# Where the block differences of a Fourier layer's first pass are made: in the Fourier layer itself, or one layer earlier on GpSimd

## The chip, the cores and the metric

The kernel runs on one core of a Trainium2 chip. The metric is the device time of one execution in microseconds; the time before is the median of three runs, 2189.78 us (2187.06 to 2193.19). One execution was profiled; it took 2191.25 us, and the span from its first to its last instruction was 2189.5 us. A change of 0.3% is 6.6 us.

## The reference, cut to what matters

Four layers follow each other on x, 2048 rows of 640 columns, in fp32: attention, Fourier, attention, Fourier. Both attention layers have the same weights, both Fourier layers the same matrices.

```python
x = x + A(layernorm(x))      # 32 heads of 20, each row sees itself and the 255 rows before it
x = x + B(layernorm(x))
x = x + A(layernorm(x))
x = x + B(layernorm(x))

def B(x):                    # real part of a Fourier transform along rows and columns
    a = x @ dft_hid_re.T
    b = x @ dft_hid_im.T
    return dft_seq_re @ a - dft_seq_im @ b
```

## The kernel before

Products in fp32 accuracy are made of three products of split operands: each operand is cut into a high part (ScalarE copies it to a rounded type) and a low part (what is left, a subtraction on VectorE or GpSimd). So every block that TensorE multiplies by costs one ScalarE and one VectorE instruction first. All DMAs are issued by SyncE, in one queue, in the order of the program text; the same holds for each engine's instructions, since the kernel is scheduled by hand.

**Attention (layers 1 and 3).** `heads` runs 128 steps, eight groups of four heads by 16 blocks of 128 rows, after a lead of ten steps. A step has two halves. In each, TensorE makes two transposed score blocks (L659) and two row-maximum score blocks (L631), VectorE reduces the latter (L636), ScalarE takes the exponent (L669), and GpSimd zeroes what lies outside the window with two selects (L675, L679). At the step's end TensorE multiplies by the values (L694), for the block whose selects ran one step earlier. Spare TensorE time is filled with the projection to queries and keys (L257). Its results are cut by GpSimd in a queue of jobs, the "pool" lane, which gives out one job each half-step (`tick`): a cast (L552) and two subtractions of 128x256 (L211) for each piece. They are stored to `qk_d` (L524) and loaded back as `qp` and `kp` (L594) some steps ahead of use; the row maxima go the same way in small DMAs (L649). Three tiles `rr` of 128x512 are first used near the end of this stage.

**Fourier (layers 2 and 4).** `seq` runs over units of the product along rows. The matrix is taken in quadrants, halves and eight blocks j of 128 rows; the first pass (half 0, part 0) has units `a1`, `a2`, `b7`, `b5`, `b` and `g`. The first ones run inside the end of the attention layer, as its output rows become ready. Each block holds column groups c0, c1, c2, c3 of 512. The pass needs three differences per block: d0 = c1 - c0, d1 = c2 - c1, d2 = c2 - d0. `load_to` loads blocks ahead, `cut_to` makes the differences and the high and low parts, `x_to` prepares the other operand, and L1415 multiplies.

In layer 2 the differences are made where they are used: `cut_to` for `a1` and `b` and for `g` with j below 3 on VectorE, for `g` from j = 3 on GpSimd (L1344); `staged` makes those of the two `b7` units, one on VectorE and one on GpSimd. So 18 are on VectorE and 6 on GpSimd. Each is then stored to `c_d` in DRAM (`keep`, 24 stores of 256 KB). In layer 4 `sums_kept` is true: nothing is subtracted, `load_to` takes the difference from `c_d` in place of the column group that only the difference needed. The flag is set at the end of the first Fourier layer.

Of the kernel before, what the change touches and what calls it, by code (L numbers as in the profile page):

```python
# [11 lines left out]
OP = mybir.AluOpType  # L12
# [11 lines left out]
NB = S // P  # L24
# [9 lines left out]
AFTER = 4  # L34
RATE = 4
FIRST = 7
LATE = 9
# [27 lines left out]
class Net:  # L65
    def __init__(self, nc, tc, ctx, a):
# [28 lines left out]
        self.cd = dram.tile([3, NB // 2, P, 512], F32, name="c_d")  # L95
        self.sums_kept = False
        self.xs = [dram.tile([S, D], F32, name=f"x_d{i}") for i in range(3)]
# [484 lines left out]
    def pack(self, quad, sb):  # L582
# [21 lines left out]
        return todo  # L604

    def heads(self, xsrc, xdst, hook):
        nc = self.nc
        qp = [t.rearrange("p (z s) -> p z s", z=2) for t in self.qp]
        kp = [t.rearrange("p (z s) -> p z s", z=2) for t in self.kp]
        pool = self.work  # L610
# [165 lines left out]
        for step in range(-LEAD, steps + 1):  # L776
# [4 lines left out]
            if step + LEAD == steps + 1:  # L781
                for b in ROLES["w"]:
                    self.ring6.pop(b, None)
            self.wide, self.lead, self.tiled = step + LEAD > steps, step < -2, step < steps - 1
            for f in later.pop(step, []):
                f()
            s, t, v = step + LEAD, step, step - 1
            if due and s >= due[0][0]:
# [3 lines left out]
                q, j = (s + AHEAD) // 16, (s + AHEAD) % 16 // 4  # L792
# [238 lines left out]
    def late(self, xsrc, xdst, hook):  # L1031
        nc = self.nc
# [29 lines left out]
        for t in range(NB):  # L1062
            sb, i = t // 4, t % 4
            y = self.y_part(t)
# [7 lines left out]
            else:  # L1072
                for hf, cs in enumerate(both):
                    p = self.bank("o", 320)
# [12 lines left out]
                out=st[1][:, 1:2], in0=st[1][:, 0:1], in1=self.half, op=OP.pow))  # L1087
# [105 lines left out]
    def take_fourier(self):  # L1193
# [6 lines left out]
        p = [cuts(t, 512) for t in self.pt]  # L1200
# [16 lines left out]
        self.acc = {}  # L1217
        self.leaving, self.keeping = [], []

# [61 lines left out]
    def staged(self, u, stage, eng=None):  # L1281

        j, out = self.order[u][3], self.cut_of.setdefault(u, [])
        p, q = cuts(self.raw_of[u], 512)
        if stage == 0:
            if not self.kept_sum(u):
                eng.tensor_tensor(out=p, in0=q, in1=p, op=OP.subtract)
                self.keep(u, p)
            return
        c = self.ring.popleft()  # L1290
        self.ring.append(c)
        self.split(c[0], c[1], (q, p)[stage - 1])
        out.append(c)
        if stage == 1:
            self.kept[j] = c

    def cut_to(self, n):
        nc = self.nc
        while self.n_cut <= min(n, len(self.order) - 1):
            u = self.n_cut  # L1300
# [3 lines left out]
            ph, j = self.order[u][2:]  # L1304
            if ph == "b7":
                if j:
                    self.staged(u, 0, nc.gpsimd)
                    self.staged(u, 1)
                    self.staged(u, 2)
# [11 lines left out]
            if ph in ("a", "a1"):  # L1321
                eng = nc.vector if ph == "a1" else nc.gpsimd
                if not self.kept_sum(u):
                    eng.tensor_tensor(out=t1, in0=q, in1=p, op=OP.subtract)  # L1324
                    if ph == "a1":
                        self.keep(u, t1)
                src = [p] + ([t1] if ph == "a" else [])
            elif ph == "a2":
                src = [t1]
            elif ph == "b5":  # L1330
                self.cut_of[u] = [self.kept.pop(j)]
                continue
            elif ph == "b":
                if not self.kept_sum(u):
                    nc.vector.tensor_tensor(out=p, in0=q, in1=p, op=OP.subtract)
                    self.keep(u, p)
# [46 lines left out]
    def seq(self, n):  # L1383
        nc = self.nc
        sb, part, ph, j = self.order[n]
        for f in self.keeping:
            f()
        self.keeping.clear()
        self.load_to(n + 3 + (ph == "a1" and len(self.raws) > 5))
# [184 lines left out]
    def fourier(self, xsrc, xdst, more):  # L1574
# [205 lines left out]
        for g in range(NB // 2):  # L1780
# [84 lines left out]
```

## Time and profile before

| | us |
|---|---|
| median of three runs | 2189.78 |
| profiled execution, whole | 2191.25 |
| its span | 2189.5 |
| TensorE busy | 2119.5 (97%) |
| VectorE busy | 1600.5 (73%) |
| ScalarE busy | 1139.8 (52%) |
| GpSimd busy | 958.5 (44%) |

Layer 1's steps run from 161 to 530 us, layer 2's products along rows from 543 to 974 us, layer 3's steps from 1252 to 1623 us, layer 4's products from 1634 to 2056 us. Engines are called PE (TensorE), DVE (VectorE), ACT (ScalarE), POOL (GpSimd) and SP (SyncE, which here only issues DMAs) in the rows. In rows of the timeline the columns are the start in us from the span's start, the length in us, engine, line, operation, the tile written and those read; what stands in brackets at the end is how long the engine was idle before, and what ended that. In rows of windows they are the stretch and its length, then for each engine its busy time and number of instructions, then the granted TensorE clock, the share of the DMA engines that was busy, and GB/s.

### The profile page before, as it was taken

Reading aid. Unit: us, or ns where it says so; the run is one execution under the profiler, and the core shown is the slowest. Engines: PE = TensorE matmul, PEld = TensorE weight load, DVE = VectorE, ACT = ScalarE, POOL = GpSimd, SP = SyncE. Lnnn points to the kernel's source line nnn. Section 1 sums busy time; section 2 is a strip of 40 time slices with the busy share of each in tenths; the row PEclk is TensorE's granted clock in tenths of the full one; section 3 lists DMA queues with packets and bytes.
Section 4 is the critical chain, followed back from the end, with each engine's and each line's share of the span. In section 5 each row is a group of like instructions: output and inputs, shape, how many; then the busy total and the mean of one; then the engine's idle time right before and its main releaser. Section 6 shows DMA issues by size and latency. Waiting matters only on the chain.

```text
span 2189.5 us, 48923 instructions
## 1 busy us (share of the span) xinstructions
PE 2119.5 (97%) x17872; PEld 1785.8 (82%) x17872; DVE 1600.5 (73%) x3931; ACT 1139.8 (52%) x2125; POOL 958.5 (44%) x1562
## 2 busy tenths in 40 slices
PE   7999999898999999999999999998999999999999
PEld 7987777677878888889999877776778888888899
DVE  6358888786897868786661588887867968687766
ACT  3117777656554545452341277776566645455332
POOL 3037776765513232332330376767655023241324
PEclk9999999999999999999999999999999999999999
DMA  5546666785566454656646566667855454546653
GB/s 183 175 156 190 199 180 210 213 222 172 200 192 188 129 183 140 212 185 200 205 156 177 161 187 196 186 204 208 216 165 180 141 187 135 166 152 209 225 166 126
DMA packets 227088, 398.40 MB, mean 182 GB/s; under 512 B 39968, under 2 KB 86560, under 8 KB 226848
## 3 DMA queue, kind: packets, MB, share of 16 engines
q1 hardware_dynamic: 226848, 395.28, 57.8%
q8 instruction: 141, 2.31, 0.5%
q14 instruction: 99, 0.81, 0.1%
HBM read 273.94 MB, written 120.06 MB: 180 GB/s over the span
## 4 chain that ended last, share of the span: by engine, by line
PE 79%; DVE 6%; DMA 4%; ACT 4%; POOL 3%; issue 2%; SPq 1%; ACTq 0%; DVEq 0%; POOLq 0%
PE banks L1415 29%; PE banks L239 15%; PE banks L257 12%; PE banks L694 6%; PE banks L659 5%; PE banks L1703 5%; PE banks L631 5%; DVE banks L636 1%; DMA qp<-qk_d 1%; ACT pt L669 1%; DVE qp L232 1%; PE banks L341 1%; DMA qk_d<-c 1%; ACT big L1038 1%; SPq L594 1%
## 5 line engine op out<-in xcount | busy, mean ns | idle before, releaser
L636 DVE CUSTOM_DVE_ANT_0 banks<-banks,mask 128x384 f32<-128x384 f32 (+2 forms) x1024 | 527.1, 556 | 121.4 <-PE banks L631 98.6
L669 ACT ACTIVATE pt<-banks 128x768 f32<-128x768 f32 (+2 forms) x512 | 393.5, 771 | 170.7 <-PE banks L659 59.8
L675 POOL TENSOR_SCALAR_AFFINE_SELECT pt<-pt 128x256 f32<-128x256 f32 x512 | 213.8, 418 | 220.3 <-ACT pt L669 201.6
L257 PE MATMUL banks<-big,wc 64*128 64x512 f32 x1920 | 271.4, 394 | 0.4 <-DVE pt L442 0.4
L659 PE MATMUL banks<-qp,kp 61*128 61x384 f32 (+2 forms) x1024 | 211.4, 382 | 24.2 <-DVE mc L636 17.0
L631 PE MATMUL banks<-kp,qp 60*128 60x384 f32 (+2 forms) x1024 | 206.9, 348 | 8.8 <-DVE mc L636 8.5
L694 PE MATMUL banks<-pt,vq 128*32 128x128 f32 x5760 | 211.2, 278 | 3.5 <-ACT pt L669 3.5
L257 PEld LDWEIGHTS banks<-big,wc 64*128 64x128 f32 x1920 | 187.3, 186 | 22.2 <-ACT x L544 1.3
L679 POOL TENSOR_SCALAR_AFFINE_SELECT pt<-pt 128x256 f32<-128x256 f32 x448 | 193.8, 433 | 0.0
L226 ACT ACTIVATE qp<-pt 128x512 fp32r<-128x512 f32 (+1 forms) x200 | 123.1, 625 | 129.3 <-DVE pt L1346 50.2
L232 DVE TENSOR_TENSOR qp<-pt,qp 128x512 fp32r<-128x512 f32 (+1 forms) x198 | 156.3, 797 | 40.9 <-ACT qp L226 39.3
L694 PEld LDWEIGHTS banks<-pt,vq 128*32 128x32 f32 x5760 | 142.2, 110 | 51.5 <-issue 36.2
L659 PEld LDWEIGHTS banks<-qp,kp 61*128 61x128 f32 x1024 | 108.6, 185 | 88.8 <-DVE mc L636 65.8
L1415 PE MATMUL banks<-qp,big 128*128 128x512 f32 x648 | 153.6, 391 | 0.1
L631 PEld LDWEIGHTS banks<-kp,qp 60*128 60x128 f32 x1024 | 124.7, 187 | 33.7 <-DVE mc L636 21.8
L1344 POOL TENSOR_TENSOR pt<-pt,pt 128x512 f32<-128x512 f32 x32 | 46.2, 1445 | 232.5 <-DMA pt<-c 146.0
L226 ACT ACTIVATE c<-pt 128x512 fp32r<-128x512 f32 x146 | 90.4, 625 | 108.2 <-POOL pt L1324 56.4
L636 DVE DVE_READ_ACCUMULATOR2_ANT mc<- 128x1 f32 x1024 | 144.3, 141 | 0.0
L1415 PEld LDWEIGHTS banks<-qp,big 128*128 128x128 f32 x648 | 120.8, 188 | 24.9 <-POOL qp L232 0.9
L232 DVE TENSOR_TENSOR c<-pt,c 128x512 fp32r<-128x512 f32 x144 | 116.6, 813 | 26.7 <-ACT c L226 24.1
L1415 PE MATMUL banks<-qp,xc 128*128 128x512 f32 x480 | 118.2, 394 | 3.6 <-DVE xc L232 2.1
L552 POOL CAST c<-x 128x512 fp32r<-128x512 f32 x64 | 38.9, 611 | 166.5 <-ACT x L544 162.3
(253 smaller groups left out, 4477.0 us busy)
## 6 DMA issues: line engine op xcount, KB each, us to landing
pt<-c SPq DMA_DIRECT2D x166, 512.0 KB
qk_d<-c SPq DMA_DIRECT2D x80, 512.0 KB
kp<-qk_d SPq DMA_DIRECT2D x384, 80.0 KB
qp<-qk_d SPq DMA_DIRECT2D x384, 80.0 KB
kp<-u_d SPq DMA_DIRECT2D x32, 640.0 KB
o_d<-ou SPq DMA_DIRECT2D x64, 256.0 KB
x_d<-x SPq DMA_DIRECT2D x48, 320.0 KB
v_d<-pt SPq DMA_DIRECT2D x16, 768.0 KB
```

Source lines behind the costliest of these rows:

```text
L226: nc.scalar.activation(hi, src, AF.Copy, scale=-1.0 if neg else 1.0)
L232: (eng or nc.vector).tensor_tensor(out=lo, in0=src, in1=hi.bitcast(F32), op=OP.subtract)
L239: self.nc.tensor.matmul(p, x, y, start=n == 0, stop=n == last)
L257: self.nc.tensor.matmul(ps[a], x[r], y[r], start=half + i == 0, stop=half == 1 and i == n - 1, skip_group_check=True)
L631: nc.tensor.matmul(p, qp[quad % 2][b:b + 60, z, qb * P:(qb + 1) * P], kp[quad % 2][b:b + 60, z, k0 * P:(qb + 1) * P], start=True, stop=True)
L636: nc.vector.tensor_tensor_reduce(out=p, in0=p, in1=self.mask[:, 384 - n * P:], scale=1.0, scalar=NEG, op0=OP.add, op1=OP.max, accum_out=mc ...
L659: nc.tensor.matmul(self.banks[:, banks[e], :n * P], kp[quad % 2][b:b + 61, z, kb * P:(kb + 1) * P], qp[quad % 2][b:b + 61, z, kb * P:(kb + ...
L669: nc.scalar.activation(pt[quad, kb][:, 2 * z:2 * z + 2, :n * P], self.banks[:, b0:b1 + 1, :n * P], AF.Exp, scale=SCALE)
L675: nc.gpsimd.affine_select(out=t[:, :, 0:P], in_=t[:, :, 0:P], pattern=[[0, 2], [1, P]], compare_op=OP.is_ge, fill=0.0, base=0, channel_mul ...
L679: nc.gpsimd.affine_select(out=t[:, :, 256:384], in_=t[:, :, 256:384], pattern=[[0, 2], [-1, P]], compare_op=OP.is_gt, fill=0.0, base=0, ch ...
L694: nc.tensor.matmul(self.banks[32 * h:32 * h + 32, bank, :P], vq[:, 96 * (kb % 4) + 21 * h:96 * (kb % 4) + 21 * h + 32], t[:, h, (qb - kb) ...
L1415: nc.tensor.matmul(self.banks[:, bk, :], p, b[q], start=start and m == 0, stop=stop and last and m == 2, skip_group_check=True)
```

## The change

`differences_at` is new and is called at the start of each step of `heads`. In layer 1 (`ready` is 0 there) and for steps 0 to 79, ten steps are a turn and each turn serves one block j: at its steps 0, 1 and 2 it loads c0, c1, c2 into the three `rr` tiles (256 KB each), at step 4 it puts six subtractions of 128x256 into the pool lane, which make d0, d1 and d2 in place, and at step 8 it stores the three to `c_d`. Layer 2 then does what layer 4 did before: `kept_sum` no longer asks for the flag, `keep` and its stores are gone, `staged` has two stages in place of three, and the `a2` units load d0.

```diff
+TURN = 10
+    def differences_at(self, step):
+
+        j, at = divmod(step, TURN)
+        if not (0 <= j < NB // 2 and self.ready == 0):
+            return
+        c = self.rr
+        if at < 3:
+            self.nc.sync.dma_start(c[at], self.a["c"][0, 0, j][:, at * 512:(at + 1) * 512])
+        elif at == 4:
+            for out, x, y in ((0, 1, 0), (1, 2, 1), (2, 2, 0)):
+                for cs in (slice(0, 256), slice(256, 512)):
+                    self.job("pool", "cd", lambda out=out, x=x, y=y, cs=cs: self.nc.gpsimd.tensor_tensor(
+                        out=c[out][:, cs], in0=c[x][:, cs], in1=c[y][:, cs], op=OP.subtract))
+        elif at == 8:
+            self.flush("cd")
+            for k in range(3):
+                self.post(k, lambda k=k: self.nc.sync.dma_start(self.cd[k, j], c[k]))
...
             self.wide, self.lead, self.tiled = step + LEAD > steps, step < -2, step < steps - 1
+            self.differences_at(step)
...
-                self.post(3, lambda u=u: self.staged(u, 0, nc.vector))
-                self.post(6, lambda u=u: self.staged(u, 1))
-                self.post(9, lambda u=u: self.staged(u, 2))
+                self.post(6, lambda u=u: self.staged(u, 0))
+                self.post(9, lambda u=u: self.staged(u, 1))
...
     def kept_sum(self, u):
-        return self.sums_kept and self.order[u][:2] == (0, 0)
-
-    def keep(self, u, t):
-
-        sb, part, ph, j = self.order[u]
-        if not self.sums_kept and sb + part == 0:
-            kind = {"a1": 0, "b": 1, "b7": 1, "g": 2}[ph]
-            self.keeping.append(lambda: self.nc.sync.dma_start(self.cd[kind, j], t))
+        return self.order[u][:2] == (0, 0)
...
             if ph in ("a", "a1"):
-                eng = nc.vector if ph == "a1" else nc.gpsimd
-                if not self.kept_sum(u):
-                    eng.tensor_tensor(out=t1, in0=q, in1=p, op=OP.subtract)
-                    if ph == "a1":
-                        self.keep(u, t1)
+                if ph == "a":
+                    nc.gpsimd.tensor_tensor(out=t1, in0=q, in1=p, op=OP.subtract)
...
                 if not self.kept_sum(u):
                     nc.vector.tensor_tensor(out=p, in0=q, in1=p, op=OP.subtract)
-                    self.keep(u, p)
...
-                eng = nc.vector if self.order[u][:2] == (0, 0) and j < 3 else nc.gpsimd
                 if self.kept_sum(u):
                     t1, p = p, t1
                 else:
-                    eng.tensor_tensor(out=t1, in0=p, in1=t1, op=OP.subtract)
-                    self.keep(u, t1)
+                    nc.gpsimd.tensor_tensor(out=t1, in0=p, in1=t1, op=OP.subtract)
...
-        self.ready, self.hid, self.sums_kept = 8, False, True
+        self.ready, self.hid = 8, False
```

Two places show what moves. The first is GpSimd's queue in layer 1, at step 5, before. `pt` is the tile with the exponents, L675 and L679 are the two selects, L552 and L211 are the jobs for one piece of the projection (`x` its raw copy, `c` its parts).

```order
L552 CAST c<-x 128x512
L675 AFFINE_SELECT pt_96<-pt_96 128x2x128
L679 AFFINE_SELECT pt_96<-pt_96 128x2x128
L211 TENSOR_TENSOR c<-x,c 128x256
L675 AFFINE_SELECT pt_96<-pt_96 128x2x128
L679 AFFINE_SELECT pt_96<-pt_96 128x2x128
L211 TENSOR_TENSOR c<-x,c 128x256
L675 AFFINE_SELECT pt_97<-pt_97 128x2x128
L679 AFFINE_SELECT pt_97<-pt_97 128x2x128
```

And the same place with the change, where L693 and L697 are the selects and L617 the new subtractions on the `rr` tiles:

```order
L552 CAST c<-x 128x512
L693 AFFINE_SELECT pt_96<-pt_96 128x2x128
L697 AFFINE_SELECT pt_96<-pt_96 128x2x128
L617 TENSOR_TENSOR rr_101<-rr_102,rr_101 128x256
L693 AFFINE_SELECT pt_96<-pt_96 128x2x128
L697 AFFINE_SELECT pt_96<-pt_96 128x2x128
L617 TENSOR_TENSOR rr_101<-rr_102,rr_101 128x256
L693 AFFINE_SELECT pt_97<-pt_97 128x2x128
L697 AFFINE_SELECT pt_97<-pt_97 128x2x128
L617 TENSOR_TENSOR rr_102<-rr_103,rr_102 128x256
```

The new jobs stand one to a half-step, between the selects. In this turn the two subtractions that finish the piece come six half-steps later than before. In each of the eight turns the six new jobs stand directly beside the six jobs of two projection pieces, so that twelve half-steps in a row carry a job, where six did.

The second place is VectorE in layer 2's first pass, units `b` with j = 2 and 3, before. L1335 is the difference, L232 writes low parts (`qp`, `rr`, `c`), L1174 and L1175 make sums of the other operand.

```order
L1335 TENSOR_TENSOR pt_97<-pt_97 128x512
L232 TENSOR_TENSOR qp_105<-pt_97,qp_105 128x512
L232 TENSOR_TENSOR c<-pt_97,c 128x512
L232 TENSOR_TENSOR rr_8425<-big_6078,rr_8425 128x128
L232 TENSOR_TENSOR qp_8428<-s_7213,qp_8428 128x256
L232 TENSOR_TENSOR qp_8428<-kp_8060,qp_8428 128x256
L1174 TENSOR_TENSOR big_5880<-big_5880 128x256
L1175 TENSOR_TENSOR kp_8060<-big_6078,big_5880 128x256
L1335 TENSOR_TENSOR pt_95<-pt_95 128x512
```

And with the change (L1192 and L1193 are those sums):

```order
L232 TENSOR_TENSOR qp_105<-pt_97,qp_105 128x512
L232 TENSOR_TENSOR c<-pt_97,c 128x512
L232 TENSOR_TENSOR rr_8514<-big_6174,rr_8514 128x128
L232 TENSOR_TENSOR qp_8517<-s_7309,qp_8517 128x256
L232 TENSOR_TENSOR qp_8517<-kp_8145,qp_8517 128x256
L1192 TENSOR_TENSOR big_5976<-big_5976 128x256
L1193 TENSOR_TENSOR kp_8145<-big_6174,big_5976 128x256
L232 TENSOR_TENSOR rr_8516<-pt_95,rr_8515 128x512
```

One instruction of each unit is gone, and the rest keeps its order. TensorE's own order is the same in both kernels from end to end.

More of the change, by code (lines that the diff above doesn't have):

```diff
@@ L95, in __init__ @@
         self.cd = dram.tile([3, NB // 2, P, 512], F32, name="c_d")
-        self.sums_kept = False
         self.xs = [dram.tile([S, D], F32, name=f"x_d{i}") for i in range(3)]
@@ L1217, in take_fourier @@
         self.acc = {}
-        self.leaving, self.keeping = [], []
+        self.leaving = []
     def take_rest(self):
@@ L1271, in kept_sum, with staged @@
     def kept_sum(self, u):
-        return self.sums_kept and self.order[u][:2] == (0, 0)
-    def keep(self, u, t):
-        sb, part, ph, j = self.order[u]
-        if not self.sums_kept and sb + part == 0:
-            kind = {"a1": 0, "b": 1, "b7": 1, "g": 2}[ph]
-            self.keeping.append(lambda: self.nc.sync.dma_start(self.cd[kind, j], t))
-    def staged(self, u, stage, eng=None):
+        return self.order[u][:2] == (0, 0)
+    def staged(self, u, stage):
         j, out = self.order[u][3], self.cut_of.setdefault(u, [])
         p, q = cuts(self.raw_of[u], 512)
-        if stage == 0:
-            if not self.kept_sum(u):
-                eng.tensor_tensor(out=p, in0=q, in1=p, op=OP.subtract)
-                self.keep(u, p)
-            return
         c = self.ring.popleft()
         self.ring.append(c)
-        self.split(c[0], c[1], (q, p)[stage - 1])
+        self.split(c[0], c[1], (q, p)[stage])
         out.append(c)
-        if stage == 1:
+        if stage == 0:
             self.kept[j] = c
@@ L1306, in cut_to @@
                 if j:
-                    self.staged(u, 0, nc.gpsimd)
+                    self.staged(u, 0)
                     self.staged(u, 1)
-                    self.staged(u, 2)
                 continue
@@ L1335, in cut_to @@
                     nc.vector.tensor_tensor(out=p, in0=q, in1=p, op=OP.subtract)
-                    self.keep(u, p)
                 src = [q, p]
@@ L1385, in seq @@
         sb, part, ph, j = self.order[n]
-        for f in self.keeping:
-            f()
-        self.keeping.clear()
         self.load_to(n + 3 + (ph == "a1" and len(self.raws) > 5))
```

1 line of the change is left out of this document (removed).

## The prediction

> **What bounds the kernel now.** First the page's busy shares and the chain that ended last:
>
> ```profile
> PE 2119.5 (97%) x17872; PEld 1785.8 (82%) x17872; DVE 1600.5 (73%) x3931; ACT 1139.8 (52%) x2125; POOL 958.5 (44%) x1562
> PE 79%; DVE 6%; DMA 4%; ACT 4%; POOL 3%; issue 2%; SPq 1%; ACTq 0%; DVEq 0%; POOLq 0%
> ```
>
> TensorE bounds the whole, and the change touches none of its instructions. So it can only gain where TensorE waits or runs slowly for VectorE, and only lose where the moved work makes it wait.
>
> The program holds its own comparison. Layer 4's first pass already runs without subtractions, and with the change layer 2's has the same instructions on every engine. So I cut the pass at the same TensorE instructions in both layers: the first `a1` product, the last one that shares TensorE with attention, the first `b` product of j = 2, the first `g` product, and `g` of j = 2. The windows of layer 2, then of layer 4:
>
> ```profile
> 543.26:594.39 51.13, 48.37 (x266) 42.95 (x265) 43.74 (x117) 28.62 (x53) 28.38 (x36) 1.00 0.68 229
> 594.39:613.65 19.26, 16.63 (x69) 11.91 (x67) 15.95 (x34) 10.81 (x26) 8.14 (x8) 1.00 0.31 101
> 613.65:635.78 22.13, 22.13 (x91) 16.52 (x91) 21.44 (x49) 12.14 (x31) 0.00 (x0) 1.00 0.67 212
> 635.78:649.82 14.04, 12.00 (x44) 8.79 (x42) 12.67 (x19) 9.51 (x18) 1.83 (x1) 0.88 0.61 191
> ...
> 1633.85:1683.07 49.22, 48.11 (x267) 43.05 (x266) 41.20 (x112) 28.73 (x53) 28.34 (x36) 1.00 0.65 213
> 1683.07:1700.77 17.70, 16.16 (x68) 12.16 (x67) 13.64 (x32) 10.87 (x27) 6.54 (x7) 1.00 0.36 108
> 1700.77:1721.62 20.85, 20.70 (x92) 16.83 (x90) 19.74 (x46) 14.42 (x34) 0.00 (x0) 1.00 0.56 174
> 1721.62:1731.14 9.52, 9.52 (x44) 7.89 (x42) 7.90 (x14) 6.98 (x14) 0.00 (x0) 1.00 0.48 143
> ```
>
> The second number is the stretch's length. In the third stretch VectorE is busy 21.44 of 22.13 us in layer 2: it sets the pace there, and the same products take 20.85 us in layer 4. The waits of the first and last stretches, from TensorE's timeline in layer 2 and in layer 4:
>
> ```profile
> 569.61 2.02 PE L239 MATMUL banks<-qp,kp 128*128 128x320 f32 x12 [1.75 <-DVE x L1077]
> 638.50 1.62 PE L1415 MATMUL banks<-qp,vq 128*128 128x512 f32 x6 [0.53 <-ACT kp L1481]
> 642.89 3.79 PE L1415 MATMUL banks<-qp,xc 128*128 128x512 f32 x9 [1.39 <-ACT xc L226]
> ...
> 1658.29 2.02 PE L239 MATMUL banks<-qp,kp 128*128 128x320 f32 x12 [0.64 <-DVE x L1077]
> ```
>
> Layer 4 has the first one shorter, 0.64 in place of 1.75 us, and the other two not at all. Layer 2's last stretch also ran at a mean granted clock of 0.88.
>
> **What the change removes.** Stretch by stretch, layer 2 less layer 4: 51.13 - 49.22 = 1.91, 19.26 - 17.70 = 1.56, 22.13 - 20.85 = 1.28, 14.04 - 9.52 = 4.52; together 9.27 us. Of the 4.52, some 0.12 x 14.04 = 1.7 us is the slower clock, the rest waits. As a check, one of the 18 subtractions on VectorE and the instruction after it:
>
> ```profile
> 611.98 0.69 DVE L1335 TENSOR_TENSOR pt<-pt 128x512 f32<-128x512 f32 x1
> 612.64 0.69 DVE L232 TENSOR_TENSOR qp<-pt,qp 128x512 fp32r<-128x512 f32 x1
> ```
>
> One occupies VectorE from 611.98 to 612.64, so 18 x 0.66 = 11.9 us leave it, against 93.80 - 82.47 = 11.3 us by the sums of the windows. That 9.27 of about 11.9 us reach TensorE is plausible, since VectorE is the late one in all four stretches. The 24 stores also leave layer 2; its loads keep their bytes. I take all 9.27. The low bound of the gain is the third stretch alone, 1.28 us, the only one in which VectorE is visibly full; the high bound is the 11.9 us.
>
> No row tells that the waits made the clock fall; layer 4, without them, shows 1.00 at the same products, so I count the 1.7 us as gained and keep the other case as a rival. The Trainium skill, TensorE: Matmul & The Clock Gate, Part 1, says that the clock falls to half after an idle window of about 3.4 us. By that rule waits of at most 1.39 us would not be the cause, the dip could stay, and the sum would be 1.7 us less.
>
> **What it adds in layer 1: GpSimd.** All in the stretch of steps 1 to 79, 166 to 380 us. Its window, then GpSimd's groups there:
>
> ```profile
> 166.00:380.00 214.00, 211.46 (x3013) 161.16 (x3012) 176.94 (x668) 155.00 (x286) 153.03 (x356) 1.00 0.63 194
> ...
> L675 POOL TENSOR_SCALAR_AFFINE_SELECT pt<-pt 128x256 f32<-128x256 f32 x158 | 64.2, 406 | 60.3 <-ACT pt L669 56.2 <-PE banks L694 2.6 <-PE banks L659 0.9
> L211 POOL TENSOR_TENSOR c<-x,c 128x256 fp32r<-128x256 f32 x40 | 29.6, 739 | 0.0
> ```
>
> The 48 new jobs have L211's shape: 48 x 0.739 = 35.5 us, so GpSimd goes from 153 to 188.5 of 214 us (88%). What hides them is its idle time of 60.3 us before L675. Whether it does so at each place, GpSimd's timeline shows, a stretch with jobs:
>
> ```profile
> 217.48 0.41 POOL L675 TENSOR_SCALAR_AFFINE_SELECT pt<-pt 128x256 f32<-128x256 f32 x1
> 217.84 0.41 POOL L679 TENSOR_SCALAR_AFFINE_SELECT pt<-pt 128x256 f32<-128x256 f32 x1
> 218.21 0.74 POOL L211 TENSOR_TENSOR c<-x,c 128x256 fp32r<-128x256 f32 x1
> 218.91 0.41 POOL L675 TENSOR_SCALAR_AFFINE_SELECT pt<-pt 128x256 f32<-128x256 f32 x1
> 219.26 0.73 POOL L679 TENSOR_SCALAR_AFFINE_SELECT pt<-pt 128x256 f32<-128x256 f32 x1
> 219.95 0.61 POOL L552 CAST c<-x 128x512 fp32r<-128x512 f32 x1
> 220.50 0.40 POOL L675 TENSOR_SCALAR_AFFINE_SELECT pt<-pt 128x256 f32<-128x256 f32 x1
> ```
>
> Counted from start to start, a subtraction takes 0.70, a cast 0.55 to 0.6, and each select 0.36. Twelve half-steps in a row now carry jobs: 24 x 0.36 + 10 x 0.70 + 2 x 0.6 = 16.8 us. TensorE gives them 12 x 214 / 158 = 16.3 us (L675 stands once in each half-step). So GpSimd falls up to 0.6 us behind in each turn, and recovers in the four free steps. The selects' reader is L694, one step later. The tightest place, a group's first block, on GpSimd and on TensorE:
>
> ```profile
> 208.21 0.41 POOL L675 TENSOR_SCALAR_AFFINE_SELECT pt<-pt 128x256 f32<-128x256 f32 x1 [0.52 <-ACT pt L669]
> 209.93 0.42 PE L694 MATMUL banks<-pt,vq 128*32 128x128 f32 x8
> ```
>
> The select ends at 208.62, its reader starts at 209.93: 1.3 us in hand against 0.6 lost. Cost: nothing. Without that cover each turn would cost its lag.
>
> What is late next is a projection piece whose jobs wait six half-steps, about 8 us; its store and the loads after it move with it. That takes us to the queue.
>
> **What it adds in layer 1: DMAs.** 24 loads and 24 stores of 256 KB, 12.6 MB over 214 us, 59 GB/s beside 194. Of SyncE's timeline and waits:
>
> ```profile
> 209.73 0.48 SPq L712 DMA_DIRECT2D o_d<-ou  x1
> 213.91 1.09 SPq L649 DMA_DIRECT2D qp<-mt  x2
> 380.78 1.40 SPq L649 DMA_DIRECT2D qp<-mt  x2
> ...
> SPq L649 <- ACT mt L647: 16.0, 11, 2.4
> ...
> GB/s 187 107 241 203 174 147 282 217 193 118 241 217 169 98 286 222 179 125 248 208 194 87 273 250 206 82 258 185 190 112 228 272 185 125 263 193 207 67 223 286
> ```
>
> The sum of 253 GB/s is below the 286 that single slices reach. Issuing them costs 48 x 0.48 = 23 us of SyncE's time, 0.5 us for each DMA that stands ahead of another. Behind the three stores of a turn stand the small `mt` loads and the `qp` loads. For `mt` SyncE itself waited in eleven cases, 16.0 us in all, so as a rule it is ahead. The readers on TensorE of the two `mt` above start here:
>
> ```profile
> 221.77 0.44 PE L659 MATMUL banks<-qp,kp 61*128 61x384 f32 x2 [0.23 <-DVE mc L636]
> 384.73 0.44 PE L659 MATMUL banks<-qp,kp 61*128 61x384 f32 x2 [0.36 <-DMA qp<-qk_d]
> ```
>
> So 221.77 - 215.0 = 6.8 us are in hand as a rule, and 384.73 - 382.2 = 2.5 us at the worst place, less the landing. Three stores ahead take 1.4 us from it, and a projection store of 1.09 us leaves the place ahead of it. Low bound 0; high bound 2 us per turn, if a store's whole landing came ahead of `mt` each time, 16 us. I take 0.5 us, near the low end, since one place of eight is tight.
>
> **The sum.** Against the profiled execution, 2191.25 us (span 2189.5): -9.27 + 0 + 0.5 = -8.8, that is 2182.5. The median of the runs is 1.5 us lower than that execution, so 2189.8 - 8.8 = **2181 us**, 0.4% faster. Layer 4 and layer 3 do the same as before and only start earlier.
>
> **The rivals.**
> - *The clock dips all the same.* Then 9.27 - 1.7 = 7.6 us are gained, less 0.5: 2182.7. For it: the waits are short. Against it: the mean of 1.00 in layer 4.
> - *Only VectorE's own pace is gained.* The waits of the last stretch end on ScalarE by the rows above. If that stretch gives nothing, 9.27 - 4.52 = 4.75 remain, less 0.5: 2185.5. Against it: layer 4 has none of these waits with the same ScalarE work.
> - *The DMAs show.* SyncE's head waits for a slow store in half of the turns, 1 us each and 2 us more at the tight place: 6 us back, 2186.5. For it: 253 of 286 GB/s leaves little room.
> - *GpSimd falls behind* (slower). In the fence above a select took 0.73 instead of 0.41 at 219.26. If the new jobs stretched as much, 0.32 each, a turn would lose 0.6 + 12 x 0.32 = 4.4 us, of which 1.3 are covered: 3.1 x 8 = 25 us back, 2206. It decides from a job of about 0.75 us start to start: (16.3 - 8.6) / 12 = 0.64 is free, and 1.3 / 12 = 0.11 more is in hand. Against it: the 40 such jobs of this stretch have a mean of 739 ns in all, 0.70 from start to start.
> - *The change does nothing*: excluded, the order shows the subtractions gone.
>
> The Trainium skill, GPSIMD Engine Reference, section 1, says GpSimd shares its SBUF interfaces with VectorE and contends with VectorE instructions that read two SBUF inputs. In these steps VectorE mostly reduces scores out of PSUM (L636, with one mask in SBUF), so by that rule too such stretching stays rare.
>
> **How the numbers follow.** Forecast 0.55, the clock's dip 0.10, VectorE's pace only 0.12, DMAs 0.15, GpSimd 0.08. The forecast's own spread is some 3 us either way, from the clock, which may dip elsewhere, and from runs that spread by 6 us. The range takes in the three middle rivals and leaves out the slower one: 2176 to 2189. A change of 0.3%, 6.6 us, is about what can be told from none; that bound is 2183.2. Of the forecast's 0.55 about 0.47 lies beyond it, of the dip's 0.10 0.06, of the other two 0.04 each: faster 0.61, the same 0.31, slower 0.08.
>
> **What would show it.** Right: layer 2's first pass from its first `a1` product to `g` of j = 2 in about 97.3 us; no clock below 1.00 there; layer 1 from the first to the 80th step within 1 us of now; GpSimd near 188 us in that window. Wrong: L694 waiting for GpSimd, L659 for `qp<-mt`, or L552 in layer 1 waiting for a store.

## The result, and the profile after

The changed kernel takes 2201.86 us (median of four runs, 2201.24 to 2203.23) against 2188.68 for the kernel before (four runs, 2187.06 to 2193.19): a ratio of 1.0054, 95% interval 1.0035 to 1.0072. It is slower by half a per cent, where 0.4% faster was forecast. The profiled execution took 2201.24 us, 9.99 more than that of before.

The busy shares and the chain that ended last, from the page of the changed kernel:

```profile
PE 2120.5 (96%) x17872; PEld 1788.6 (81%) x17872; DVE 1582.6 (72%) x3913; ACT 1140.6 (52%) x2125; POOL 979.9 (45%) x1604
PE 74%; DMA 8%; DVE 6%; ACT 4%; POOL 4%; issue 3%; SPq 2%; ACTq 0%; DVEq 0%; POOLq 0%
```

VectorE lost 17.9 us of work, as meant. The chain shows the other side: TensorE's share fell from 79% to 74%, that of DMA rose from 4% to 8%.

Layer 2's first pass, in the windows between the same TensorE instructions as before (length, then busy time of PE, PEld, DVE, ACT, POOL, the clock, DMA share, GB/s):

```profile
566.90:615.45 48.55, 47.91 (x267) 43.05 (x265) 40.45 (x110) 28.46 (x53) 27.74 (x36) 1.00 0.65 212
615.45:633.28 17.83, 16.17 (x68) 12.16 (x67) 13.63 (x32) 11.01 (x27) 6.68 (x7) 1.00 0.32 107
633.28:654.13 20.85, 20.70 (x92) 16.82 (x90) 19.83 (x46) 14.42 (x34) 0.00 (x0) 1.00 0.54 171
654.13:663.65 9.52, 9.52 (x44) 7.89 (x42) 7.90 (x14) 6.98 (x14) 0.00 (x0) 1.00 0.51 150
```

Together 96.75 us, against 106.56 before: the gain is 9.8 us in these two executions, and the clock is at 1.00 throughout. The loss is in layer 1. Its stretch from the first score product of step 0 to that of step 80, before and after:

```profile
161.18:379.48 218.30, 214.90 (x3038) 163.63 (x3036) 181.03 (x683) 157.15 (x288) 156.32 (x363) 1.00 0.63 194
...
161.58:399.31 237.73, 223.29 (x3038) 169.75 (x3037) 181.31 (x683) 157.22 (x288) 187.98 (x411) 0.96 0.73 225
```

The same 3038 products take 19.4 us more, and the mean granted clock is 0.96. TensorE's longest waits there, in total, times and longest, before (166 to 380 us) and after (166 to 400 us), then three stretches of the changed kernel that follow the long ones:

```profile
PE banks L659 <- DVE mc L636: 2.3, 8, 0.4
...
PE banks L677 <- DMA qp<-mt: 10.3, 4, 3.1
...
238.10:241.50 3.40, 3.40 (x19) 2.69 (x22) 1.71 (x7) 1.35 (x2) 1.47 (x3) 0.50 0.71 212
320.00:326.80 6.80, 6.21 (x49) 5.24 (x51) 1.67 (x11) 2.57 (x5) 2.92 (x6) 0.50 0.78 197
357.50:364.40 6.90, 6.14 (x41) 4.97 (x43) 2.56 (x9) 2.57 (x5) 3.10 (x7) 0.51 0.65 174
```

Before, no product waits for `mt` there. After, score products wait four times for `qp<-mt`, 10.3 us, and there are 17.1 us at half the clock right behind three of these waits, which cost some 8.5 more (half of 17.1; TensorE's busy time grew by 8.4): 18.8 of the 19.4. The first of these waits, on ScalarE, SyncE and TensorE, and the issue and the reader of the same piece before the change:

```profile
226.11 0.25 ACT L665 ACTIVATE mt<-banks 16x128 fp32r<-16x128 f32 x1
...
232.77 1.33 SPq L667 DMA_DIRECT2D qp<-mt  x2
...
237.61 0.44 PE L677 MATMUL banks<-qp,kp 61*128 61x384 f32 x2 [3.09 <-DMA qp<-mt]
...
225.14 1.10 SPq L649 DMA_DIRECT2D qp<-mt  x2
...
232.42 0.44 PE L659 MATMUL banks<-qp,kp 61*128 61x384 f32 x2
```

`mt` is finished at 226.36 and issued at 232.77: it is 6.4 us behind. Before the change the same piece had 6.2 us in hand (232.42 - 226.24), out of which its landing had to come: here the score starts 3.5 us after the issue's end. SyncE's own waits for `mt` show that this is no single accident; they were 16.0 us in eleven cases before:

```profile
SPq L667 <- ACT mt L665: 2.8, 2, 1.9
```

In nearly every group of steps SyncE now arrives late. What is lost by step 80 grows to 23.2 us at the start of layer 2; 9.8 come back there. The last 3.8 aren't shown to be the change's: l2_only below, which adds nothing to layer 1, loses 3.9 between step 80 and layer 2 as well. Layer 3 took 3.6 us less than in the profiled execution before, mostly at steps 96 to 104, where the clock fell in that one and not in this; I put this part down to the run and not to the change, since layer 3's instructions are the same.

### The profile page after: what moved, and what is told of

Its sections match the earlier page's. It is cut to its first block, busy times and chain, and to the rows that moved or that the text cites. A ratio compares the mean times of both kernels' runs of the same rounds, so it can differ in the third digit from the quotient of the medians.

```text
span 2199.5 us, 49035 instructions
## 1 busy us (share of the span) xinstructions
PE 2120.5 (96%) x17872; PEld 1788.6 (81%) x17872; DVE 1582.6 (72%) x3913; ACT 1140.6 (52%) x2125; POOL 979.9 (45%) x1604
## 4 chain that ended last, share of the span: by engine, by line
PE 74%; DMA 8%; DVE 6%; ACT 4%; POOL 4%; issue 3%; SPq 2%; ACTq 0%; DVEq 0%; POOLq 0%
PE banks L1411 30%; PE banks L239 14%; PE banks L257 11%; PE banks L1699 5%; PE banks L712 5%; PE banks L677 4%; PE banks L649 4%; DMA qp<-qk_d 1%; DMA qk_d<-c 1%; DMA qp<-mt 1%; ACT pt L687 1%; DVE banks L654 1%; DMA rr<-r_d 1%; POOL pt L693 1%; SPq L594 1%
## 5 line engine op out<-in xcount | busy, mean ns | idle before, releaser
L654 DVE CUSTOM_DVE_ANT_0 banks<-banks,mask 128x384 f32<-128x384 f32 (+2 forms) x1024 | 527.2, 557 | 140.5 <-PE banks L649 117.3
L693 POOL TENSOR_SCALAR_AFFINE_SELECT pt<-pt 128x256 f32<-128x256 f32 x512 | 213.9, 418 | 204.7 <-ACT pt L687 183.7
L712 PE MATMUL banks<-pt,vq 128*32 128x128 f32 x5760 | 211.4, 278 | 3.5 <-ACT pt L687 3.5
L697 POOL TENSOR_SCALAR_AFFINE_SELECT pt<-pt 128x256 f32<-128x256 f32 x448 | 191.4, 427 | 0.0
L232 DVE TENSOR_TENSOR qp<-pt,qp 128x512 fp32r<-128x512 f32 (+1 forms) x197 | 155.6, 797 | 40.4 <-ACT qp L226 39.0
L712 PEld LDWEIGHTS banks<-pt,vq 128*32 128x32 f32 x5760 | 142.3, 110 | 51.5 <-issue 35.8
L232 DVE TENSOR_TENSOR c<-pt,c 128x512 fp32r<-128x512 f32 x146 | 115.3, 793 | 26.1 <-ACT c L226 23.6
L1328 POOL TENSOR_TENSOR pt<-pt 128x512 f32<-128x512 f32 x30 | 42.7, 1424 | 161.5 <-DVE pt L1345 99.8
```

Of the source, the lines that this page charges most:

```text
L232: (eng or nc.vector).tensor_tensor(out=lo, in0=src, in1=hi.bitcast(F32), op=OP.subtract)
L654: nc.vector.tensor_tensor_reduce(out=p, in0=p, in1=self.mask[:, 384 - n * P:], scale=1.0, scalar=NEG, op0=OP.add, op1=OP.max, accum_out=mc ...
L693: nc.gpsimd.affine_select(out=t[:, :, 0:P], in_=t[:, :, 0:P], pattern=[[0, 2], [1, P]], compare_op=OP.is_ge, fill=0.0, base=0, channel_mul ...
L697: nc.gpsimd.affine_select(out=t[:, :, 256:384], in_=t[:, :, 256:384], pattern=[[0, 2], [-1, P]], compare_op=OP.is_gt, fill=0.0, base=0, ch ...
L712: nc.tensor.matmul(self.banks[32 * h:32 * h + 32, bank, :P], vq[:, 96 * (kb % 4) + 21 * h:96 * (kb % 4) + 21 * h + 32], t[:, h, (qb - kb) ...
```

## The experiments

Theories: **A**, SyncE's queue falls behind with the added transfers; **B**, GpSimd's subtractions hold up the projection's pieces and the stores; **C**, only both together. "Stretch" is the time from step 0's first score to step 80's, against 218.30 before. "Behind" is the mean, over the 16 `mt` of steps 16 to 79, of the time from the end of `mt` on ScalarE to its first issue; it was 0.09 us before. Single times stand beside one run of the kernel before on the same chip. Where that is 2189.28, it is the median of 23 runs.

**The two halves apart.**

> The kernel before with all of the added work in layer 1 (24 loads, 48 subtractions, 24 stores, these into a DRAM tensor of its own), while layer 2 still makes its own differences. If the two halves of the change are independent, layer 1's steps 0 to 96 lose 22 us or so against before (21 to 24, as the changed kernel's trace has it), layer 2's first pass gains nothing, and the time is about 2189 + 23 = 2212 us. If the loss needs layer 2's changed form, the time stays near 2190.

```
 # the kernel before, plus differences_at as in the change, storing to
+self.ed = dram.tile([3, NB // 2, P, 512], F32, name="e_d")
```

2214.19 against 2188.85. Stretch +22.5; layer 2's first pass took 104.9 us, 1.6 us shorter than before, about what the fall of the clock there had cost: its last stretch took 12.40 us in place of 14.04, at a clock of 1.00, although the differences are still made in it.

> The changed kernel without any of the added work in layer 1; layer 2 and layer 4 load blocks of the cosine matrix where the differences would stand (so the output is another one, the bytes loaded are the same). Theory: layer 2's gain stands by itself, 9 to 10 us: 2179 to 2181 us. Rival: part of the 9.9 us that layer 2 gained after the change is only a recovery of what layer 1's delay had left late; then 3 to 6 us are gained, 2184 to 2187.

```
-            self.differences_at(step)
-                self.nc.sync.dma_start(self.t1[j], self.cd[0, j])
+                self.nc.sync.dma_start(self.t1[j], self.a["c"][0, 0, j][:, 512:1024])
-                    self.nc.sync.dma_start(p, self.cd[1 + (ph == "g"), j])
+                    self.nc.sync.dma_start(p, self.a["c"][0, 0, j][:, 0:512])
```

This kernel multiplies by other blocks, so its output is another one. 2182.21 against 2188.85, 6.6 us less, which lies between the two ranges expected. Layer 2's first pass took 9.8 us less than before, but 3.9 us were lost between step 80 and layer 2, where the clock fell twice (at 431.6 and 527.2 us) and in the profile before once (at 432.6). So the gain stands by itself, and so does the loss in the heads.

**Which part of layer 1's work.**

> The kernel before with the 24 loads and 24 stores in layer 1 alone, no subtractions (what is stored are the loaded blocks, into a DRAM tensor that nobody reads). Theory A, SyncE's queue falls behind because 48 more transfers are issued and awaited there: most of the loss, 12 to 23 us, is here, mt is issued 3 to 7 us after it is made, and scores wait for qp<-mt. Theory B, the subtractions on GpSimd delay the projection's pieces and hold the stores: under 5 us lost here. Theory C, only both together: under 5 us here and under 5 us with the subtractions alone.

```
 # l1_all without
-        elif at == 4:
-            for out, x, y in ((0, 1, 0), (1, 2, 1), (2, 2, 0)):
...
```

2214.65 against 2188.85. Stretch +18.1, behind 4.2 us: theory A.

> The kernel before with the 48 subtractions on GpSimd in layer 1 alone (on tiles that VectorE fills once), no loads and no stores. Theory A (SyncE's queue): within 2 us of before, GpSimd at about 188 us busy in the 214 us of steps 1 to 79, mt issued as soon as it is made. Theory B (GpSimd's jobs delay the pieces): 12 us or more lost. Theory C: under 5 us lost.

```
 # l1_all without the loads and stores; at step 0 instead
+            for t in c:
+                self.nc.vector.memset(t, 1.0)
```

2208.07 against 2188.85, not the 2188 of theory A; but `mt` was 0.2 us behind, so not theory B either. Of the stretch's +9.4 us, 2.9 stem from my filling of the tiles at 164 us. The rest is one stall, looked at below.

**Issues or bytes.**

> The kernel before with the same 48 transfers in layer 1 at the same places of SyncE's queue, but only 16 of the 512 columns each (8 KB instead of 256 KB); no subtractions, and nobody reads what is stored. With whole blocks the same 48 transfers cost 24.6 us up to layer 1's 96th step. Theory A1, the time that SyncE needs to issue them (0.4 to 0.5 us each, 20 us in all) puts mt late: still 15 us or more lost, mt issued 4 to 7 us after it is made. Theory A2, the bytes count (a transfer waits for the landing of the eighth before it, which large neighbours delay): under 5 us lost, mt issued under 2 us after it is made as a rule.

```
-            self.nc.sync.dma_start(c[at], self.a["c"][0, 0, j][:, at * 512:(at + 1) * 512])
+            self.nc.sync.dma_start(c[at][:, :16], self.a["c"][0, 0, j][:, at * 512:at * 512 + 16])
 # and the stores alike, in l1_dma
```

2194.19 against 2189.31. Stretch +3.2, behind 2.5 us. The issues alone use up what `mt` had in hand, but hardly more; the bytes make the larger part of the loss. It isn't the landing of `mt` itself that the bytes delay: by the trace's landing records its transfers landed 3.4 us after their issue began in both kernels (medians of the stretch; 2.9 before).

> The changed kernel with one load and one store of 768 KB for each block in place of three and three of 256 KB: 16 transfers in place of 48, the same bytes, a third of the issues and of the places in the queue. Theory A1 (issue time): most of layer 1's loss is gone, 2182 to 2188 us. Theory A2 (bytes): layer 1 still loses 15 us or more, 2195 to 2202 us.

```
-        if at < 3:
-            self.nc.sync.dma_start(c[at], self.a["c"][0, 0, j][:, at * 512:(at + 1) * 512])
+        if at == 1:
+            self.nc.sync.dma_start(self.rr_all, self.a["c"][0, 0, j][:, :1536])
 # and one store of 768 KB
```

2197.72 against 2189.31. Stretch +13.5, behind 4.1 us, with a third of the issues. How bytes reach `mt`, SyncE's timeline and its waits in this kernel show (of rows with x3, three transfers in a row):

```profile
371.55 0.40 SPq L618 DMA_DIRECT2D rr<-c  x1
372.00 1.11 SPq L599 DMA_DIRECT2D kp<-qk_d  x3
373.15 1.09 SPq L599 DMA_DIRECT2D qp<-qk_d  x3
374.35 0.34 SPq L644 DMA_DIRECT2D vq<-v_d  x1
379.09 1.07 SPq L599 DMA_DIRECT2D qp<-qk_d  x2
...
SPq L599 <- DMA rr<-c: 15.0, 6, 4.4
```

The `qp` load at 379.09 reads and writes nothing that the `rr` load touches. It is the eighth transfer after it, and SyncE stood still for 4.4 us until that one had landed. Six such waits, each eight places behind an `rr` load, make the 15.0 us. The trace's semaphore records tell why eight. All transfers of the program report their landing on eight semaphores in turn, and a transfer that waits so waits for the semaphore on which it will report itself: the `rr` load and the `qp` load at 379.09 both have number 105. So this is how the program's transfers are synchronised; no run shows the queue of the chip to have such a limit.

**Another queue.**

> The changed kernel with the two small mt transfers of each group of four steps (in layers 1 and 3) issued by ScalarE, which makes mt, instead of by SyncE. If mt's place behind others in SyncE's queue is what stops the scores, no score waits for qp<-mt any more, layer 1 takes as long as before or less, and layer 2's 9.9 us remain: 2176 to 2182 us. Rival: the queue's delay then shows at the next reader, the loads of queries and keys, or ScalarE loses 1 us per group by issuing: 2190 us or more.

> The kernel before with mt issued by ScalarE, nothing else. Control for the last one: it tells what moving mt gives without the change. Before, only one score waited for mt (1.71 us at 432.96, with a fall of the clock just after): 0 to 5 us faster, 2184 to 2189 us; if ScalarE's issuing costs exps their lead, slower, 2192 us or more.

```
-                self.post(1, lambda z=z: nc.sync.dma_start(
+                self.post(1, lambda z=z: nc.scalar.dma_start(
                     qp[quad % 2][60:125:64, z, u * 512:(u + 1) * 512].bitcast(F32),
```

2311.94 and 2281.87 against 2189.31. In the latter `mt` is never behind, and yet:

```profile
181.44 1.08 ACTq L649 DMA_DIRECT2D qp<-mt  x2
...
183.50 0.38 PE L631 MATMUL banks<-kp,qp 60*128 60x256 f32 x1 [1.10 <-ACT pt L669]
```

The two issues occupy ScalarE for 1.08 us, and in each group of steps TensorE waits up to 1.1 us for the exp behind them. The queue is freed, at an engine that has less to spare than SyncE. TensorE's waits in the changed kernel with that edit, from 166 to 440 us:

```profile
PE banks L649 <- DVE mc L654: 24.3, 10, 5.2
PE banks L649 <- ACT pt L687: 16.1, 19, 1.1
```

No score waits for `mt` any more; nineteen waits for ScalarE and ten for VectorE's reductions have come up in their place: the rival of the expectation, and worse.

> The kernel with 16 transfers of 768 KB, these now issued by ScalarE, so that none of them stands in SyncE's queue and no transfer of SyncE's waits for the landing of one of them as the eighth before it. Bytes on the DMA engines unchanged. Theory A2a, the large transfers hold up SyncE's queue itself: mt is issued under 1.5 us after it is made, layer 1 loses 0 to 10 us (0.5 us of ScalarE for each issue), 2181 to 2190 us. Theory A2b, the DMA engines are so full that every transfer lands late whatever queue it is in: mt still 4 us or more behind, 2195 us or more.

```
-            self.nc.sync.dma_start(self.rr_all, ...
+            self.nc.scalar.dma_start(self.rr_all, ...
 # and the store alike, in wide
```

2241.38 against 2192.84. Neither theory: `mt` was 6.0 us behind, more than with SyncE. SyncE's waits:

```profile
SPq L599 <- DMA rr<-c: 25.7, 5, 6.9
SPq L672 <- DMA c_d<-rr: 17.7, 3, 7.1
```

SyncE waits up to 7.1 us for transfers that ScalarE issues and whose data its own don't touch. The transfers of both queues report on the same eight semaphores, and in each of these eight cases SyncE waited for the semaphore of a transfer that ScalarE had issued. So this run doesn't separate the two theories.

**Fewer bytes in the heads.**

> The change for the g differences alone: 24 loads, 32 half-width subtractions and 8 stores in layer 1's heads, that is 8.4 MB in place of 12.6 MB; layer 2 makes the differences for a1 and b itself as before, and loads those for g. If the loss grows with the bytes (theory A2) and there is slack to be used up first, layer 1 loses half as much as in the changed kernel or less, 5 to 12 us, and layer 2's last stretch gains 4 to 5: 2190 to 2197 us. If the loss belongs to each turn however large, 16 us or more are lost: 2201 us.

```
+        return self.order[u][:2] == (0, 0) and (self.sums_kept or self.order[u][2] == "g")
 # differences_at: three loads, (0, 1, 0) and (2, 2, 0), one store of c[2]
```

2204.16 against 2192.84, above the range expected. Stretch +11.5 for two thirds of the bytes, behind 3.5 us; layer 2 gains 3.0 us, where 4 to 5 were expected.

> The change for blocks 0 to 3 alone, a turn every 20 steps, its transfers one by one two or three steps apart: 24 transfers and 6.3 MB in layer 1's heads; blocks 4 to 7 are made by layer 2 as before. SyncE's theory: before, its only spare time in these steps are the 16.0 us that it waits for mt. 24 transfers of 0.45 us are 11 us, less than that, so the queue does not fall behind for good: layer 1 loses 0 to 4 us, layer 2 gains 5 to 7, 2183 to 2189 us. If any such transfer costs the same, half of 22 us is lost: 2195 us.

```
-TURN = 10
+TURN = 20
+        return self.order[u][:2] == (0, 0) and (self.sums_kept or self.order[u][3] < 4)
 # loads at 0, 3, 6; subtractions from 9; stores at 14, 16, 18; blocks 0 to 3 alone
```

2190.99 against 2189.28, ratio 1.0002 (0.9991 to 1.0014). Stretch +2.4, behind 2.0 us, one wait of 2.2 us for `mt`; layer 2 gains 6.2. The loss per byte falls from 1.5 us per MB (19.4 for 12.6 MB) and 1.4 in g_heads (11.5 for 8.4 MB) to 0.4 (2.4 for 6.3 MB). That fits a backlog that must first fill up the spare time better than a price for each transfer; but half_heads also issues its transfers two or three steps apart, and no run separates their number from their spacing. The 0 to 4 us expected for the heads hold up to step 80. Another 5.7 are lost from there to layer 2, where `mt` is 2 to 8 us behind in the kernel before already; how much of that is the backlog's and how much the clock's, these runs don't tell.

**Subtractions without pauses.**

> As l1_sub (48 subtractions on GpSimd in the heads, no transfers), but the tiles are filled by GpSimd before layer 1's first step, so that the 2.5 us which that fill cost at 164 us are gone. There one subtraction of VectorE (wc<-x,wc, both inputs in SBUF, 0.58 us elsewhere) took 4.96 us at 352.36 while GpSimd ran without a pause from 340 to 357 us. If GpSimd without pauses keeps VectorE from such an instruction, this comes again in the turn from step 60 to 70 or another: one such instruction over 1.5 us and 3 to 7 us lost by step 96. If that was an accident: under 1 us lost, 2188 to 2191 us.

```
 # l1_sub, the tiles filled ahead of layer 1's heads
+            for t in self.rr:
+                nc.gpsimd.memset(t, 1.0)
```

2194.84 against 2189.28. Stretch +6.7, all of it here, on VectorE and then GpSimd:

```profile
348.15 4.98 DVE L213 TENSOR_TENSOR wc<-x,wc 128x384 fp32r<-128x384 f32 x1
353.06 0.55 DVE L654 CUSTOM_DVE_ANT_0 banks<-banks,mask 128x384 f32<-128x384 f32 x1
...
351.25 0.42 POOL L693 TENSOR_SCALAR_AFFINE_SELECT pt<-pt 128x256 f32<-128x256 f32 x1
351.61 0.42 POOL L697 TENSOR_SCALAR_AFFINE_SELECT pt<-pt 128x256 f32<-128x256 f32 x1
351.99 0.74 POOL L213 TENSOR_TENSOR c<-x,c 128x256 fp32r<-128x256 f32 x1
357.47 0.41 POOL L693 TENSOR_SCALAR_AFFINE_SELECT pt<-pt 128x256 f32<-128x256 f32 x1 [4.75 <-ACT pt L687]
```

VectorE's subtraction with both inputs in SBUF took 4.98 us, 0.58 elsewhere, and ended 0.4 us after GpSimd's row of work ran out at 352.73. TensorE waited 4.2 us for the scores' reduction behind it, and the clock stood at half for 6.8 us from 353.6 on, which makes the rest.

> As l1_sub2, but the subtractions are handed out one in each step, at every other half-step, instead of one in each half-step; their number stays 48, only six half-steps with a subtraction never stand in a row ahead of the six of a projection piece, so that GpSimd gets pauses there. Twice VectorE's wc<-x,wc at the end of the seventh turn took 4.96 and 4.98 us and ended 0.3 us after GpSimd's run without a pause ended. If that run is what kept VectorE from it, no such instruction takes over 1.5 us here, and layer 1 is within 1 us of before at its 96th step: about 2189 us. If the subtractions cost VectorE something by their number alone, such an instruction comes again and 5 to 7 us are lost.

```
-        if at == 4:
-            for out, x, y in ((0, 1, 0), (1, 2, 1), (2, 2, 0)):
+        if 2 <= at < 8:
+            out, x, y = ((0, 1, 0), (1, 2, 1), (2, 2, 0))[at // 2 - 1]
 # one half-width subtraction in each of the steps 2 to 7 of a turn
```

2183.28 (the kernel before beside it 2193.42; its single runs spread from 2185.57 to 2196.89, so the 10 us say little). Stretch -0.5, and the same instruction:

```profile
346.46 0.56 DVE L213 TENSOR_TENSOR wc<-x,wc 128x384 fp32r<-128x384 f32 x1
```

With pauses the 48 subtractions cost the stretch nothing in this run. The SBUF — State Buffer page of the Trainium skill, section "Who interferes with whom", says that a VectorE instruction with two SBUF inputs contends with a GpSimd instruction that reads SBUF, and that the ports they share are an exclusive lock. These runs fit that: the VectorE instruction is the one held. That it got no turn between GpSimd's instructions, ten of which started in that time, goes beyond what the section says.

**The same work before the heads.**

> As the last one, but the g differences are made before layer 1's heads, between 74 and 125 us, where the trace shows GpSimd idle for 60 us and nothing on TensorE that waits for mt. If the loss is only a matter of mt's place behind late transfers in the heads, nothing is lost here and layer 2's last stretch gains 4 to 5 us: 2184 to 2187 us. Rival: the transfers make the loads of queries and keys late at the start of the heads: 2190 us or more.

> All 24 differences made before layer 1's heads, between 74 and 125 us: 48 transfers and 12.6 MB there, none in the heads; layer 2 as in the changed kernel. By the same theory the full 9 to 10 us of layer 2 are gained, 2179 to 2182 us. Against it: 12.6 MB in 50 us are 250 GB/s beside the 160 that flow there, more than the 307 that the 224 GB/s at a busy share of 0.73 in the changed kernel's heads make for all engines; if the overflow, 50 to 60 us x 100 GB/s, delays the start of the heads, 5 to 20 us are lost and it ends at 2185 to 2200 us.

> Blocks 0 to 3 alone, made between 69 and 115 us, before the heads; nothing is added to the heads. 6.3 MB in 45 us, 140 GB/s beside 160: within what the DMA engines carry. Layer 1 loses 0 to 1 us, layer 2 gains 5 to 7 us: 2183 to 2185 us. Rival: layer 2's gain needs the differences of all eight blocks; then 2188 us.

> All eight blocks before the heads as in early_all, but spread from 64 to 115 us with four sets of tiles, loads up to four blocks ahead. In early_all the heads began 8.1 us late, after loads that waited behind these transfers. Starting 13 us sooner gives the DMA engines some 13 us x 140 GB/s = 1.8 MB more room, of the 5 or so that were too many: the heads begin 3 to 6 us late, layer 2 gains 9: 2182 to 2186 us.

```
+    def early(self):
+        sets = [cuts(self.pt[2], 512), cuts(self.pt[3], 512), self.rr, self.ou + [self.vq[2]]]
+        for n, (load, cut, store) in enumerate(EARLIER):
...
+                nc.gpsimd.tensor_tensor(out=c[out], in0=c[x], in1=c[y], op=OP.subtract)
 # called after each value block and piece from 64 us on; early_all, early_g: three sets, from 74 us;
 # early_half: only blocks 0 to 3, kept_sum as in half_heads
```

Only g: 2190.41 against 2192.84, nothing lost in the heads, 2.6 us gained in layer 2, where 4 to 5 were expected. All from 74 us on: 2188.09 against 2192.84; the heads' stretch is as before, but they begin 8.1 us late. Two rows of VectorE and TensorE in that run:

```profile
135.79 1.66 DVE L211 TENSOR_TENSOR wc<-x,wc 128x384 fp32r<-128x384 f32 x1 [6.15 <-ACT wc L219]
138.24 1.06 PE L651 MATMUL banks<-kp,qp 60*128 60x384 f32 x2 [5.12 <-DVE mc L656]
```

The weights' chunk `wc` is late: its load was issued at 128.66, behind the added transfers. Blocks 0 to 3 alone: 2184.82 against 2189.28, ratio 0.9979 (0.9968 to 0.9989). All eight, from 64 us on with four sets of tiles: **2181.73 us, ratio 0.9959 (0.9946 to 0.9972)**, faster than both kernels. The window of its transfers, and its heads:

```profile
64.00:125.00 61.00, 59.55 (x374) 55.96 (x373) 17.15 (x36) 10.49 (x25) 30.22 (x25) 1.00 0.92 310
...
162.18:380.36 218.18, 214.75 (x3038) 163.67 (x3036) 181.06 (x683) 157.17 (x288) 156.33 (x363) 1.00 0.63 194
```

The DMA engines are busy to 0.92 there, against 0.73 in the changed kernel's heads, and TensorE runs through (59.55 of 61.00 us), since nothing that it needs soon stands behind the transfers. The heads begin 1.0 us late and take 218.18; layer 2 gains 9.8.

## Why the prediction was wrong

- **What is removed** was right in its size: 9.27 us forecast, 9.8 measured, in each stretch within 0.7 us of layer 4's figure. Whether the 1.7 us of clock belong to it, the 1.00 in layer 2's last stretch doesn't tell: the same stretch is at 1.00 in l1_all, l1_dma, l1_sub, l1_tiny, l1_sub2 and l1_sub3, which still make the differences there. Over the whole pass, the clock fell for 3.4 us in seven of the eight profiles with the old pass, at various places, and in one of the seven in which layer 2 makes none. Without a fall on either side (l1_all 104.9 us, the changed kernel 96.75) the gain is 8.2 us. So the clock's part, up to 1.6 us, mostly comes with the change, but not as a fixed amount.
- **GpSimd** was right for the changed kernel: 187.98 us busy in the stretch (188.5 in a slightly shorter one were forecast), and no `L712` product (the old L694) waits for it. But the cover was thinner than I said. I asked whether selects and pieces come late, and set the rule on shared SBUF interfaces that I cited from the Trainium skill (GPSIMD Engine Reference, section 1) aside because VectorE mostly reads PSUM there. One instruction in each projection chunk does not, and in two runs of the subtractions alone it was held for 5 us. In l1_all it took 1.58 us, in the profiled changed kernel 0.61; that the stalls for `mt` had shifted it there is my reading, not shown.
- **The DMA term** is the step that failed: 0.5 us were taken for it, and 19.4 were lost by step 80. I took "0.5 us for each DMA that stands ahead of another" and set it against the 6.8 us in hand of a single `mt`. The delays don't stand each for itself, they add up in a queue. The same part had 23 us of issuing and 16.0 us in which SyncE waited for `mt`, the largest of its waits and the part of its slack that keeps `mt` on time. 23 is more than 16, so the queue falls behind until TensorE waits: in the changed kernel `mt` is 1.7, 4.5, 5.5 and 6.4 us behind in four groups in a row, then comes the wait of 3.09 us, and then it starts anew at 0.3. l1_tiny shows the issues alone: behind 2.5 us, stretch +3.2. Two smaller slips: the landing was named but not taken from the 6.8 us, and the "projection store of 1.09 us" is the row of two `mt` loads; a projection store (L524) takes 0.39 us in the median.
- **The landings** of the added bytes, the larger part of that term, stand in the high bound of 16 us and in a rival, but not in the 0.5 us. I compared the sum of 253 GB/s with 286 and found room. l1_dma against l1_tiny gives the bytes 14.9 of the 18.1 us. In l1_dma's stretch SyncE waited 14 times, 9.1 us in all, for the landing of an added transfer, in l1_tiny never; in the changed kernel's 17 times, 10.0 us. The loads of `qp` also landed later, 4.1 us after their issue began in l1_dma and 3.4 in l1_tiny (medians). How the 14.9 us divide between the two stays open.
- **The clock** stands in the sum as a gain only. Here it made 10.3 us of waits into 18.8.
- **The rivals.** "The DMAs show" had the mechanism (SyncE's head behind a slow transfer, `mt` late) and 6 us for it; 19.4 were lost by step 80. The term's high bound, 2 us in each of eight turns or 16 us, would have given 2196.5 and the right direction. I kept it out of the range by treating one place of eight as tight. "GpSimd falls behind", the slower rival that I named, did not happen.

## What to carry to other kernels

An in-order queue is an engine: before you add transfers to it, compare their issue time plus the waits for older transfers with the queue's own idle time, read from what it waits for, not with the slack of the one transfer behind them. Work with many bytes belongs where nothing urgent stands behind it in the queue, even if the DMA engines are fuller there. And before GpSimd is filled up, look for VectorE instructions with two inputs in SBUF, and leave pauses for them.

## What the hardware showed that was not expected

- SyncE stopped until the eighth transfer before had landed, whatever it carried, and also for transfers that ScalarE issued (up to 7.1 us). The semaphore records put this down to the program's eight landing semaphores, not to the chip.
- Issuing two transfers of 4 KB cost ScalarE 1.08 us.
- Row after row of GpSimd instructions, none longer than 0.76 us, held one VectorE instruction for 4.96 and 4.98 us.
- The clock fell to half behind single waits of 2.7 to 3.1 us. The Trainium skill, TensorE: Matmul & The Clock Gate, Part 1, has an idle window of about 3.4 us for it; these waits are shorter, so the measurement decides. The wait of 1.4 us, the fourth of the 10.3, had no fall behind it. But no threshold follows for a single wait: in l1_tiny the clock fell behind one of 1.93 us and not behind one of 1.92, and in the profile before it fell at 644.3 us, where the waits are at most 1.39 us.
